# Two fused layers after attention: the next batch's attention laid beside the first product instead of the second, and weights converted in another order

## The chip, the cores and the metric

The kernel runs on one core of a Trainium2 chip. Its time is the device time of one execution in microseconds (us); the time before is 1533.37 us, the median of three runs (1531.82 to 1533.52). Engines: TensorE (PE) multiplies matrices into PSUM banks, VectorE (DVE) and ScalarE (ACT) do elementwise work, GpSimd (POOL) and SyncE (SP) here mostly issue DMAs. Each engine runs its instructions in order; between engines there are semaphores.

## The reference

Attention without softmax for 8 batches of 8 heads, 576 positions, 64 wide; then each row is divided by its root mean square and scaled by g. The result, as 4608 tokens of 512 values, goes through two layers with a hidden width of 2048:

```python
kv = np.einsum('bhsd,bhse->bhde', k, v)
out = np.einsum('bhsd,bhde->bhse', q, kv)
rms = np.sqrt(np.mean(out * out, axis=-1, keepdims=True) + 1e-06)
x = (out / rms * g_norm)                      # reshaped to (4608, 512)
h = x @ w_in;  x = (h * sigmoid(1.702 * h)) @ w_out      # layer 1
h = x @ w2_in; x = (h - np.tanh(h)) @ w2_out             # layer 2
```

All of it is float32.

## The kernel before

**Groups.** The tokens are worked in eight groups of 576, and a group of layer 1 is one batch of the attention. A group has two stages: `m1` (M1, x times W_in, activation) and `m2` (M2, times W_out). Both compute a product of 2x2 blocks by seven products of sums of blocks (the letter r in the code), so x, the weights and the hidden values are needed in seven forms. Each number is split in a high and a low float16, and each product is three matrix products (high-high, high-low, low-high). M1 has 54 steps of six matrix products of 288 columns, and two more steps of it (the tails) stand behind the first two steps of M2; M2 has 28 steps of twelve. Groups 0 and 1 of layer 1 use plain products (`m1_plain`, and `m2_plain` for group 0), while the weights of layer 1 are still being converted.

**Work on the other engines.** In M1 ScalarE copies bank X to `mscratch` (L664) and applies the activation (L638, L642), and VectorE adds the banks Y and Z to the copies (L669). For M2 the hidden values become operands `jt`: sums on VectorE (L692), the high part on ScalarE (L706), the low part on VectorE (L712), up to seven operands ahead of TensorE. At the end of a product M2 scales bank X (ScalarE, L760) and adds Y or Z (VectorE, L754); results go to memory from `mscratch`, which has room for six buffers of 288 columns. The weights of M2 stream in on SP's queue.

**Side work.** Besides that there are generators, from which `tick` takes pieces: after each step of M1 or M2 a generator's rate is added up, and for each full 1 its next piece (up to a `yield`) is put into the program. `drain` takes what is left. TensorE and SP run in the written order; the order on the other engines is decided by the scheduler, by its own estimates, no earlier than the marks at which a piece was put in. The generators are:

- `front(b)`: the attention products of batch b on TensorE (k times v, L425; times q, L434; the sums of squares, L441) with ScalarE's copies, squares (L467) and scaled copies (L468), then the roots (`roots`, L507 and L508, with a change of ScalarE's function table and back).
- `back(b)`: two steps on the roots (`newton`, L513 and L514), the roots out to memory (L556) and back, spread over 64 partitions each (L564), the multiplication (L571), then `xprep`: x in seven forms (L336), high parts (ScalarE, L346), low parts (VectorE, L349), into `xo[b % 2]`.
- `conv1`: 32 items, W_out of layer 2 first (16 items), then W_in. An item loads raw words (GpSimd's queue, L144 and L145), makes float32 of them (ScalarE L156, then VectorE L159 to L162), sums (L171 to L174), high parts (ScalarE, L224, 896 columns), low parts (VectorE, L177) and stores them (L229, L232). Two raw buffers take turns.
- `x2load`: x of layer 2, read back and prepared by the same `xprep`.

k, v and q of a batch come by GpSimd's queue (L380): k and v into a region with room for one piece of 1280 words, so the next of four pieces waits for the products that read the one before.

**Where they stand.** In M1 of group n (2 to 6) runs `back(n+1)` at 0.5, in M2 of groups 2 to 5 `front(n+2)` at 0.75; group 1 has all of batch 2 and the products of batch 3. `conv1` begins in M2 of group 2 at 0.85 and runs from group 3 at 0.62 in M1 and 0.5 in M2; it must be drained ahead of M2 of group 7, where `reload` brings W_in of layer 2 in. GpSimd's queue issues in order: the loads of k and v, the roots and the conversion's loads and stores all pass it.

## Time and profile before

| | us |
|---|---|
| median of three runs | 1533.37 |
| profiled execution | 1537.64 |
| its span | 1535.7 |
| PE busy in it | 1441.6 (94%) |
| DVE busy | 1159.7 (76%) |
| ACT busy | 892.7 (58%) |

The profile is one execution; its stages can be told apart by the lines of the products (L631 to L633 in M1, L817 to L819 in M2). A row of the table of stages gives the stretch, its length and the busy time of each engine in it; a row of the order of time gives start, duration, engine, line, operation, and in brackets how long the engine had been idle and what released it. PEclk is the mean granted clock of TensorE as a share of its higher level. Busy time of TensorE counts the pipelined ends of its products, so what a gap costs is best read from a stage's length.

### The profile page before, as it was taken

To read this page: it belongs to the slowest core of one execution; us is meant where nothing else is said; L and a number is where in the kernel's file an instruction comes from. 1 tells how busy PE (TensorE), PEld (TensorE's weight loads), DVE (VectorE), ACT (ScalarE), POOL (GpSimd) and SP (SyncE) were. 2 spreads that over 40 slices of the span, in tenths; PEclk is the share of its full clock that TensorE was granted. 3 is DMA by queue.
4 is the path that set the end of the run, shared out by engine and by line. 5 is a ranking of instruction groups with operands and counts; after the bars stand their busy time and mean duration, and the time that the engine had idled before them with its cause. 6 is when DMAs were issued, how large, how long until landed. Compare 5 with 4: busy or idle time off the path is not lost.

```text
span 1535.7 us, 29954 instructions
## 1 busy us (share of the span) xinstructions
PE 1441.6 (94%) x11922; PEld 1112.7 (72%) x11922; DVE 1159.7 (76%) x2237; ACT 892.7 (58%) x1871; POOL 152.5 (10%) x238
## 2 busy tenths in 40 slices
PE   6999978998899889998999999999999999999999
PEld 5667756676666666766777777777777777777777
DVE  3998878394885976967978686887778787868585
ACT  5775554664765756747656564645565555656463
POOL 0001010102322222111110000000000000000000
PEclk9999999999999999999999999999999999999999
DMA  8776836437477387384586516061523334240504
GB/s 285 220 239 192 249 92 203 129 115 249 125 238 226 90 269 225 124 287 131 178 292 228 181 34 222 14 203 39 171 85 132 124 104 136 71 154 31 194 15 155
DMA packets 104684, 247.55 MB, mean 161 GB/s; under 512 B 10624, under 2 KB 55296, under 8 KB 104544
## 3 DMA queue, kind: packets, MB, share of 16 engines
q1 hardware_dynamic: 83504, 161.49, 32.6%
q0 software_dynamic: 21040, 84.15, 17.4%
q8 instruction: 93, 1.52, 0.4%
q14 instruction: 47, 0.39, 0.1%
HBM read 202.62 MB, written 42.98 MB: 160 GB/s over the span
## 4 chain that ended last, share of the span: by engine, by line
PE 45%; DVE 19%; issue 19%; DMA 11%; ACT 5%; POOL 1%; SPq 0%; DVEq 0%; ACTq 0%; POOLq 0%
PE X L817 4%; PE X L818 4%; PE X L819 4%; PE X L631 3%; PE X L632 3%; PE X L633 3%; DVE gt L692 3%; DVE jt L712 3%; DMA scratch<-rd 2%; PE Y L817 2%; PE Y L819 2%; PE Y L818 2%; PE Z L631 2%; PE Z L633 2%; PE Z L632 2%
## 5 line engine op out<-in xcount | busy, mean ns | idle before, releaser
L706 ACT ACTIVATE jt<-gt 128x576 f16<-128x576 f32 x420 | 284.5, 682 | 179.7 <-PE X L819 73.6
L712 DVE SCALAR_TENSOR_TENSOR jt<-gt,jt 128x576 f16<-128x576 f32 x420 | 312.9, 753 | 95.9 <-ACT jt L706 92.8
L817 PE MATMUL X<-jt,st 128*128 128x288 f16 x960 | 278.6, 290 | 16.8 <-ACT mscratch L760 14.8
L818 PE MATMUL X<-jt,st 128*128 128x288 f16 x960 | 278.4, 290 | 3.7 <-DVE jt L712 3.7
L819 PE MATMUL X<-jt,st 128*128 128x288 f16 x960 | 278.1, 290 | 0.0
L631 PE MATMUL X<-xo,wi 128*128 128x288 f16 x896 | 256.8, 287 | 19.5 <-ACT mscratch L664 17.8
L632 PE MATMUL X<-xo,wi 128*128 128x288 f16 x896 | 256.8, 287 | 0.0
L633 PE MATMUL X<-xo,wi 128*128 128x288 f16 x896 | 256.7, 286 | 0.0
L632 PEld LDWEIGHTS <-wi 128*128 128x128 f16 x1568 | 153.6, 98 | 83.1 <-issue 43.5
L818 PEld LDWEIGHTS <-st 128*128 128x128 f16 x1680 | 165.9, 99 | 60.6 <-issue 18.5
L817 PEld LDWEIGHTS <-st 128*128 128x128 f16 x1680 | 165.8, 99 | 55.8 <-issue 11.6
L819 PEld LDWEIGHTS <-st 128*128 128x128 f16 x1680 | 165.9, 99 | 52.4 <-issue 9.1
L631 PEld LDWEIGHTS <-wi 128*128 128x128 f16 x1568 | 153.7, 98 | 41.1 <-issue 1.8
L633 PEld LDWEIGHTS <-wi 128*128 128x128 f16 x1568 | 153.7, 98 | 39.3
L664 ACT COPY mscratch<-X 128x288 f32<-128x288 f32 x336 | 130.7, 393 | 80.3 <-PE X L633 63.6
L692 DVE TENSOR_TENSOR gt<-gt 128x576 f32<-128x576 f32 x240 | 175.7, 749 | 0.6
L631 PE MATMUL Z<-xo,wi 128*128 128x288 f16 x448 | 128.3, 286 | 16.0 <-DVE mscratch L669 15.6
L818 PE MATMUL Y<-jt,st 128*128 128x288 f16 x480 | 138.1, 288 | 3.3 <-DVE jt L712 3.3
L817 PE MATMUL Y<-jt,st 128*128 128x288 f16 x480 | 138.3, 288 | 0.7 <-DVE mscratch L669 0.5
L819 PE MATMUL Y<-jt,st 128*128 128x288 f16 x480 | 138.3, 288 | 0.0
L669 DVE TENSOR_TENSOR mscratch<-Z,mscratch 128x288 f32<-128x288 f32 x224 | 101.3, 452 | 46.7 <-ACT mscratch L664 23.6
L633 PE MATMUL Z<-xo,wi 128*128 128x288 f16 x448 | 128.4, 287 | 0.0
(240 smaller groups left out, 2482.1 us busy)
## 6 DMA issues: line engine op xcount, KB each, us to landing
st<-wod SPq DMA_DIRECT2D x210, 512.0 KB, 4.8
scratch<-atp POOLq DMA_DIRECT2D x28, 640.0 KB, 6.1
scratch<-x2d SPq DMA_DIRECT2D x32, 288.0 KB, 5.6
cbk<-w_out POOLq DMA_DIRECT2D x32, 256.0 KB, 3.9
cbk<-w_in POOLq DMA_DIRECT2D x32, 256.0 KB, 3.8
scratch<-atp POOLq DMA_DIRECT2D x14, 576.0 KB, 5.5
scratch<-rd POOLq DMA_DIRECT2D x28, 288.0 KB, 6.3
x2d<-mscratch SPq DMA_DIRECT2D x28, 288.0 KB, 5.5
```

The source lines that it names most:

```text
L631: nc.tensor.matmul(out=out, lhsT=wh, rhs=xh, start=fresh and kt == 0, stop=False, skip_group_check=k)
L632: nc.tensor.matmul(out=out, lhsT=wh, rhs=xl, start=False, stop=False, skip_group_check=k)
L633: nc.tensor.matmul(out=out, lhsT=wl, rhs=xh, start=False, stop=kt == 1, skip_group_check=k)
L664: main(nc.scalar.copy(out=b.ap, in_=x))
L669: main(nc.vector.tensor_tensor(out=b.ap, in0=add[0], in1=b.ap, op=ALU.add))
L692: tt = lambda o, a, b: main(nc.vector.tensor_tensor(out=G[:, :, o, :], in0=G[:, :, a, :], in1=G[:, :, b, :], op=ALU.subtract))
L706: main(nc.scalar.activation(out=j[:, :, 0, :], in_=GT[STEPS2[i][1]][:, :, QD[STEPS2[i][0]], :], func=AF.Copy, scale=SX))
L712: main(nc.vector.scalar_tensor_tensor(out=j[:, :, 1, :], in0=GT[STEPS2[i][1]][:, :, QD[STEPS2[i][0]], :], scalar=SX, in1=j[:, :, 0, :], op ...
L817: nc.tensor.matmul(out=out, lhsT=wh, rhs=xh, start=a, stop=False, skip_group_check=k)
L818: nc.tensor.matmul(out=out, lhsT=wh, rhs=xl, start=False, stop=False, skip_group_check=k)
L819: nc.tensor.matmul(out=out, lhsT=wl, rhs=xh, start=False, stop=z, skip_group_check=k)
```

## The change

- `front` is split into `front_early` (batches 1 and 2, as before) and a new `front` for batches 3 to 7, which has the products and squares alone, with ScalarE's squares and copies in halves of 288 columns. It runs in M1 of groups 2 to 6 at 0.5 and is drained at M1's end.
- the new `back` has the roots too, and runs in M2 of groups 2 to 6 at 1.1. Group 1 has only batch 2, at 0.75 and 0.85.
- k and v of batches 3 to 7 go into the x buffer that is idle meanwhile (`xk`, room for three pieces); q has room for two pieces instead of one.
- `conv1` takes W_in first, has its high part in two halves (eight pieces per item instead of seven) and runs at 0.2 in M2 of group 2, at 0.64 and 0.2 in groups 3 to 6, at 0.85 and 0.7 in group 7, and is drained behind M1 of layer 2's first group. Only W_in's items must be done by M2 of group 7.
- `mscratch` has room for seven buffers of 288 columns; the shared scratch is 576 words smaller.

```diff
-SCRATCH, MAIN = 6472, 7 * 256
+SCRATCH, MAIN = 5896, 7 * 288
-    rx, rs, rq, rk = (Scratch(scratch[:, a:z], z - a) for a, z in
-                      ((0, 8 * H), (8 * H, 12 * H), (12 * H, 16 * H), (16 * H, SCRATCH)))
+    rx, rs, rq0, rq1, rk = (Scratch(scratch[:, a:z], z - a) for a, z in
+                            ((0, 8 * H), (8 * H, 12 * H), (12 * H, 16 * H), (12 * H, 20 * H), (16 * H, SCRATCH)))
+    xk = [Scratch(t.rearrange("p a b c d -> p (a b c d)").bitcast(F32), 14 * H) for t in xo]
+    qs_of = lambda b: rq0 if b < 3 else rq1
+    kvs_of = lambda b: rk if b < 3 else xk[b % 2]
 def conv1():
-        items = [(kind, p, h) for kind in (1, 0) for p in range(NP) for h in range(2)]
+        items = [(kind, p, h) for kind in (0, 1) for p in range(NP) for h in range(2)]
...
-            nc.scalar.copy(out=d[:, :, 0, :], in_=B[:, 1:8])
-            yield
+            for a, b in ((0, 4), (4, 7)):
+                nc.scalar.copy(out=d[:, a:b, 0, :], in_=B[:, 1 + a:1 + b])
+                yield
...
+            converted[0] += 1
-    def front(b):
+    def front_early(b):
...
+    def front(b):
+
+        kvs, qs = [ahead[b][0]], [ahead[b][1]]
+        kvs.append((yield from unit_kv(b, 1)))
+        qs.append((yield from queries(b, 1)))
+        for kt in range(2):
+            for i in range(2):
+                kb = kvs.pop(0)
+                head_products(i, kb.ap[:, 0:1280])
+                kb.free()
+                if kt == 0:
+                    kvs.append((yield from unit_kv(b, 2 + i)))
+                yield
+                yield
...
+            for j in range(2):
+                pair_numerators(qb.ap, j)
+                yield
+                for i in range(2):
+                    nc.scalar.activation(out=sq[:, i, j], in_=AT[i][:, 0:H], func=AF.Square)
+                    nc.scalar.activation(out=og[:, i, j], in_=AT[i][:, 0:H], func=AF.Copy, scale=gsc)
+                    yield
+            qb.free()
+            pair_squares(kt, ex.ap)
+            ex.free()
+            yield
+            yield
-    def back(b, dst):
+    def back_early(b, dst):
...
+    def back(b, dst):
+
+        yield
+        yield
+        yield
+        yt[:] = (yield from rq1.need(H)), (yield from rq1.need(H))
+        roots(slice(0, P))
+        nc.scalar.activation(out=dummy, in_=yt[1].ap[:, 0:1], func=AF.Gelu_apprx_sigmoid)
+        yield
+        newton(slice(0, P))
...
+        for _ in range(5):
+            yield
+        for kt in range(2):
+            o = xbs[b, kt].ap
+            nc.vector.tensor_tensor(out=o, in0=rb[kt].ap, in1=o, op=ALU.mult)
+            rb[kt].free()
+            yield
+            ex = yield from rs.need(3 * H)
+            yield from xprep(xbs[b, kt], ex, dst[:, kt])
...
-                    bk = add_side(two(), 0.85, 0.9)
+                    bk = add_side(both(2, xo[0]), 0.75, 0.85)
                 elif n < NS - 1:
-                    bk = add_side(back(n + 1, xo[(n + 1) % 2]), 0.5, 1.0)
+                    fr = add_side(front(n + 1), 0.5, 0.0)
...
             if (l, n) == (0, 3):
-                rate(later, 0.62, 0.5)
+                rate(later, 0.64, 0.2)
+            if (l, n) == (0, 7):
+                rate(later, 0.85, 0.7)
...
-                add_side(later, 0.0, 0.85)
+                add_side(later, 0.0, 0.2)
             jcap[0] = 5
+            if (l, n) == (1, 0):
+                drain([later])
             pre = [stream(l, i) for i in range(4)]
-            if l == 0 and 1 < n < NS - 2:
-                drain([bk])
-                fr = add_side(front(n + 2), 0.0, 0.75)
+            if l == 0 and 1 < n < NS - 1:
+                drain([fr])
+                bk = add_side(back(n + 1, xo[(n + 1) % 2]), 0.0, 1.1)
             if l == 0 and n == NS - 1:
-                drain([later])
+                while converted[0] < 16:
+                    next(later)
```

The order of VectorE at the multiplication by the roots of batch 5, before. It stands in M1 of group 4: L669 adds the banks, L177 and L174 are conversion, L712 is an operand's low part, L336 a form of x.

```order
L669 TENSOR_TENSOR mscratch<-Y_85,mscratch 128x288 [waits PE_49]
L174 TENSOR_TENSOR cbk<-cbk 128x128 [waits DVE_49]
L669 TENSOR_TENSOR mscratch<-Z_87,mscratch 128x288 [waits DMAHW6_49,DMAHW2_49,Activation_49]
L571 TENSOR_TENSOR scratch<-scratch 128x1152 [waits DMASW5_49,DMASW4_49]
L177 TENSOR_TENSOR cbk<-cbk 128x7x128 [waits DMASW3_49,Activation_49]
L712 SCALAR_TENSOR_TENSOR jt<-gt_73,jt 128x2x288 [waits Activation_49]
L336 TENSOR_TENSOR scratch<-scratch 128x288 [waits DVE_49]
L712 SCALAR_TENSOR_TENSOR jt<-gt_73,jt 128x2x288 [waits Activation_49]
L669 TENSOR_TENSOR mscratch<-Z_87,mscratch 128x288 [waits PE_49]
```

The same of the changed kernel, in M2 of group 4: L645 is the multiplication, L783 an operand's low part, L825 M2's addition, L162 to L165 conversion, L343 a form of x and L356 its low part.

```order
L783 SCALAR_TENSOR_TENSOR jt<-gt_75,jt 128x2x288 [waits Activation_49]
L783 SCALAR_TENSOR_TENSOR jt<-gt_76,jt 128x2x288 [waits Activation_49]
L783 SCALAR_TENSOR_TENSOR jt<-gt_73,jt 128x2x288 [waits Activation_49]
L162 TENSOR_SCALAR cbk<-cbk 128x512
L645 TENSOR_TENSOR scratch<-scratch 128x1152 [waits DMASW5_49,DMASW4_49]
L163 SCALAR_TENSOR_TENSOR cbk<-cbk 128x512 [waits DMASW3_49,DVE_49]
L783 SCALAR_TENSOR_TENSOR jt<-gt_74,jt 128x2x288 [waits Activation_49]
L825 SCALAR_TENSOR_TENSOR mscratch<-Z_86,mscratch 128x288 [waits Activation_49]
L645 TENSOR_TENSOR scratch<-scratch 128x1152 [waits DMASW7_49,DMASW6_49]
L343 TENSOR_TENSOR scratch<-scratch 128x288 [waits DVE_49]
L825 SCALAR_TENSOR_TENSOR mscratch<-Z_87,mscratch 128x288 [waits Activation_49]
```

The multiplication, and x behind it, moved from among M1's additions to among the operands of M2; seven low parts stand directly ahead of it there.

The order of ScalarE in the first half of M2 of group 4, before: L706 is an operand's high part, L443, L426 belong to the products of batch 6, L224 and L156 to conversion, L760 is M2's scaled copy.

```order
L443 ACTIVATE ms<-AT,eps 128x288 [waits PE_49]
L224 CAST cbk<-cbk 128x7x128 [waits DMASW1_49,DMASW2_49,DVE_49,Activation_49]
L706 ACTIVATE jt<-gt_74 128x2x288 [waits PE_49]
L426 COPY kv_104<-AT 128x64 [waits PE_49]
L156 ACTIVATE cbk<-cbk 128x512 [waits DMASW3_49,DMASW2_49,DVE_49]
L760 ACTIVATE mscratch<-X_82 128x288 [waits PE_49]
L760 ACTIVATE mscratch<-X_83 128x288 [waits PE_49]
```

In the changed kernel (L777 the high part, L545, L546 and L626 the roots and the way back to the activation's table, L831 the scaled copy, L159 conversion):

```order
L545 ACT_TABLE_LOAD
L545 ACTIVATE scratch<-ms 128x288
L546 ACTIVATE scratch<-scratch 128x288 [waits Activation_49]
L777 ACTIVATE jt<-gt_75 128x2x288 [waits PE_49]
L626 ACT_TABLE_LOAD
L626 ACTIVATE dummy<-scratch 128x1 [waits Activation_49]
L777 ACTIVATE jt<-gt_76 128x2x288 [waits DVE_49,PE_49]
L777 ACTIVATE jt<-gt_73 128x2x288 [waits DVE_49,PE_49]
L777 ACTIVATE jt<-gt_74 128x2x288 [waits DVE_49,PE_49]
L831 ACTIVATE mscratch<-X_82 128x288 [waits PE_49]
L831 ACTIVATE mscratch<-X_83 128x288 [waits PE_49]
```

The start of a conversion item no longer stands ahead of the scaled copies there; the roots and the two table loads do.

## Rows read from the trace of the kernel before

**Rows 1.** Busy by stretch: us, PE, PEld, DVE, ACT, POOL, PEclk, DMA share, GB/s.
```profile
146.30:272.50 126.20, 106.24 (x920) 76.85 (x919) 103.98 (x202) 64.72 (x130) 12.04 (x21) 0.97 0.62 186
272.50:380.80 108.30, 99.38 (x867) 72.11 (x866) 65.48 (x121) 62.19 (x129) 13.29 (x21) 0.95 0.51 162
380.80:691.80 311.00, 282.12 (x2402) 208.98 (x2401) 235.92 (x459) 194.34 (x396) 73.55 (x109) 0.97 0.63 197
485.90:532.50 46.60, 40.18 (x320) 31.00 (x319) 36.29 (x76) 32.97 (x75) 10.90 (x16) 1.00 0.45 133
532.50:591.80 59.30, 53.97 (x485) 38.69 (x483) 41.22 (x78) 30.95 (x56) 14.55 (x21) 0.94 0.77 249
738.50:781.10 42.60, 42.60 (x350) 34.02 (x349) 37.57 (x70) 23.97 (x41) 6.48 (x10) 1.00 0.67 214
781.10:824.70 43.60, 40.52 (x327) 31.70 (x325) 31.35 (x65) 30.12 (x72) 6.24 (x11) 1.00 0.78 276
867.30:907.20 39.90, 39.90 (x327) 31.75 (x325) 30.69 (x67) 24.28 (x61) 0.00 (x0) 1.00 0.18 56
949.80:1284.50 334.70, 330.49 (x2690) 262.89 (x2689) 257.44 (x497) 187.37 (x401) 11.42 (x16) 1.00 0.36 117
1284.50:1324.20 39.70, 39.70 (x326) 31.65 (x324) 30.63 (x67) 24.24 (x61) 0.72 (x1) 1.00 0.13 42
```

**Rows 2.** The same for the attention's bank AT alone: PE, PEld, DVE, ACT.
```profile
532.50:591.80 59.30, 7.46 (x128) 3.80 (x128) 0.46 (x1) 6.46 (x13) 0.94 0.77 249
```

**Rows 3.** Waits of PE in M2 of group 4: us, times, longest.
```profile
PE X L817 <- ACT mscratch L760: 5.3, 1, 5.3
```

**Rows 4.** Order of time of ACT around that wait.
```profile
566.70 0.66 ACT L156 ACTIVATE cbk<-cbk 128x512 f32<-128x512 f32 x1 [5.64 <-DMA cbk<-w_out]
567.26 0.70 ACT L760 ACTIVATE mscratch<-X 128x288 f32<-128x288 f32 x2
```

**Rows 5.** Busy by stretch, right behind that wait.
```profile
566.70:573.20 6.50, 5.49 (x24) 3.37 (x24) 4.39 (x10) 2.51 (x5) 1.42 (x2) 0.50 0.41 139
```

**Rows 6.** Order of time of the roots in M1 of group 4.
```profile
486.45 1.28 ACT L507 ACT_TABLE_LOAD   x1
487.75 0.44 ACT L507 ACTIVATE scratch<-ms 128x288 f32<-128x288 f32 x1
488.83 1.28 ACT L482 ACT_TABLE_LOAD   x1
...
491.62 0.56 POOL L556 DMA_DIRECT2D rd<-scratch  x1 [0.49 <-DVE scratch L514]
495.61 2.46 POOL L564 DMA_DIRECT2D scratch<-rd  x4 [3.44 <-PE Z L633]
...
501.84 1.36 DVE L571 TENSOR_TENSOR scratch<-scratch 128x1152 f32<-128x1152 f32 x1 [3.96 <-DMA scratch<-rd]
```

**Rows 7.** Waits of PE in M1 of group 4.
```profile
PE Z L631 <- DVE mscratch L669: 3.6, 2, 3.3
PE X L631 <- ACT mscratch L664: 2.6, 3, 1.4
```

**Rows 8.** VectorE by line: count, busy us, mean ns, idle before.
```profile
L712 DVE SCALAR_TENSOR_TENSOR jt<-gt,jt 128x576 f16<-128x576 f32 x420 | 312.9, 753 | 95.9 <-ACT jt L706 92.8
L336 DVE TENSOR_TENSOR scratch<-scratch 128x288 f32<-128x288 f32 x112 | 47.1, 449 | 0.2
L177 DVE TENSOR_TENSOR cbk<-cbk 128x896 f16<-128x896 f32 x32 | 34.8, 1089 | 17.0 <-ACT cbk L224 16.7
L160 DVE SCALAR_TENSOR_TENSOR cbk<-cbk 128x512 uint32<-128x512 uint32 x42 | 28.9, 688 | 0.9
L171 DVE TENSOR_TENSOR cbk<-cbk 128x128 f32<-128x128 f32 x40 | 11.4, 284 | 0.3
```

**Rows 9.** The read-back of the roots (L564), from issue to landing.
```profile
DMA to landing us min/median/max: 4.0/6.3/9.6
```

**Rows 10.** Waits of ACT from 949.8 to 1284.5 (layer 2).
```profile
ACT mscratch L664 <- DMA outT<-mscratch: 11.5, 4, 3.6
```

## What was predicted, before the changed kernel was run

> **What bounds the kernel now.** I read the table of stages first, then the waits of TensorE, then the order of time around the longest of them. Group n is the 576 tokens of turn n; M1 and M2 are its two matrix products. In the table [rows 1] the reader is to see what a stage costs when nothing holds TensorE. The first M1 of the second layer shown, 1284.5 to 1324.2, takes 39.7 us with TensorE busy all of it, and M2 of group 6 in the first layer takes 42.6 us, also without a gap. So a pair costs 82.3 us of bare products. The attention of one batch, all of which lies in M2 of group 4, adds 7.46 us of small products [rows 2].
>
> Groups 3 to 5 of the first layer take 311.0 us, 103.7 each [rows 1], where 82.3 + 7.5 = 89.8 would do: 14 us a pair are lost. Group 4 shows where. Its M1 lasts 46.6 us instead of 39.7, 6.9 too long; its M2, which holds the products of batch 6, lasts 59.3 instead of 50.1, 9.2 too long. VectorE is busy 36.29 of 46.6 and 41.22 of 59.3, ScalarE 32.97 and 30.95: neither is full, so the loss is waiting in order, not work.
>
> In M2 there is one wait of 5.3 us, of a product for ScalarE's copy [rows 3], and the order of time tells why [rows 4]: the activation that starts a conversion item (L156) stood 5.64 us for its words from memory, and the copy that TensorE needs (L760) stood behind it. The price is not 5.3 alone: in the 6.5 us after it the granted clock reads 0.50, the lower of the two levels (1.2 GHz), where TensorE had stood idle, and 24 products take 5.49 us [rows 5]; at the full level they take about 2.9 (42.60 us for 350). In M1 the roots stand at the start: two table loads of 1.28 us each with the roots between them [rows 6], behind which the copies of X come late (2.6 us, [rows 7]), and then the multiplication by the roots (L571) holds VectorE 3.96 us for the read-back [rows 6], which TensorE feels as 3.6 us [rows 7].
>
> **The change, part by part.**
>
> *Groups 2 to 6.* The products of batch n+1 go beside M1 of group n, its roots, scaling and x beside M2. Per pair the products stay 7.5 us. M1 loses the two table loads, the roots and the read-back, so the waits of [rows 6, 7] go; M2 loses the conversion's rush (0.2 pieces per step instead of 0.5, 28 steps: 5.6 pieces, under one item of 8) and the products.
>
> M1 after: VectorE gives up two multiplications of 1.36 us [rows 6], two steps of 0.45 for the roots, eight subtractions of 0.449 and x's low parts (six of 0.753, two of 0.449) [rows 8]: 12.6 us. It takes on conversion: 0.64 x 54 steps / 8 = 4.3 items where 0.62 x 54 / 7 = 4.8 were issued; nothing more. ScalarE gives up the loads, the roots and x's high parts (some 8 us) and takes the 13 instructions of [rows 2], 6.46 us, of which eight are now split in two, at some 0.1 us more a half: about 7.5. So ScalarE stays near 33 and VectorE falls below 30, in a stage that is 7.5 us longer. What is late next there is ScalarE in order: a pair's second product waits until the first one's squares and copies are out of the AT banks, one call (two steps, 1.7 us) earlier in the program. The nearest stage is M1 of group 7, 43.6 us, 3.9 over the bare 39.7, with ScalarE at 30.12 and VectorE at 31.35 [rows 1]. Bounds: 0 (M1 of group 8 has 39.9) and 6.9 (group 4). I take 3.5.
>
> M2 after: the order puts the work of the roots and of x on VectorE among 22 low parts. The sum of the wide ones is 32 x 0.753 = 24.1, ten narrow ones 4.5, the 12.6 from above, and one item of conversion: 1.089, two of 0.688, four of 0.284 and one smaller one, 4.0 [rows 8]. That is 45.2. The same sum for M2 of group 6 (32 wide, 10 narrow, 28 of conversion) gives 42.6, where the row reads 37.57 busy [rows 1], since neighbours overlap: a factor 0.88. So 40 us of 42.6: it fits, but only just, and a wait of VectorE shows. Two are added. The roots end on ScalarE some 11 us into M2 (fourth call at 1.1 per step, after the two tail steps of M1) and VectorE comes to them at about that time. Then the read-back: the write's issue of 0.56 us and its landing, four loads whose issue takes 2.46 us [rows 6], and their landing, 6.3 us in the middle and 4.0 to 9.6 at the ends [rows 9]. In M1 of group 4 the multiplication starts 10.2 us after the write's issue (501.84 - 491.62, [rows 6]); I take 10, 8 to 14. Between the end of the roots and the multiplication VectorE has 8 to 10 us of work by the order, so the wait is 0 to 2 us in the middle, 5 at the worst; queued behind it are the low parts, of which the order has six or seven in store (8 to 9 us of TensorE), and x, which the next M1 needs at once. Behind the multiplication stand some 19 us of VectorE's work, so x is complete about 24.5 + 19.2 = 43.7 us after M2's start, 1 late. Bounds: 0 (group 6) and 9.2 (group 4). I take 2.
>
> A pair is then 82.3 + 7.5 + 3.5 + 2.0 = 95.3. Groups 3 to 5: 311.0 to 285.9, -25.1. Group 2: 108.3 to 95.8 (half a microsecond more, as its x now comes late in group 1), -12.5. Group 6 had no products: 781.1 - 691.8 = 89.3 becomes 95.3, +6.0.
>
> The Trainium skill, page ScalarE: Activation LUTs, section What ACT_TABLE_LOAD costs, has a switch of tables cost about 2.66 us, a load of 1283 ns and a drain of 1380. The load agrees with this trace's 1.28 [rows 6]; the drain does not show: the root starts 0.02 us after the first load's end (487.75 against 486.45 + 1.28). By the page the two switches would put the roots 2.8 us later into M2, and each of five pairs up to that much later, 14 in all; by the rows nothing.
>
> *k and v in the idle x buffer.* Three of 1280 words fit instead of one, so the loads no longer wait in turn for the products that free the only buffer. Cost nothing: the buffer is idle until x is written, in M2. Unlike before, the loads are out before M1 starts.
>
> *Group 1.* It loses batch 3's products (7.5 us, part of them beside VectorE's backlog) and its waits for them: 126.2 to 118.0, -8.2; bounds 0 and -15, since VectorE is busy 103.98 of it [rows 1] and its floor stays.
>
> *Conversion at the end.* Pieces: 4 + 32 x 8 = 260. Up to group 6 5.6 + 4 x 40.2 = 166 are issued; M1 of group 7 takes 46, its M2 20, and the rest, 28, falls to M1 of the second layer's first group. M1 of group 7: 31.35 + (5.7 - 2) x 4.0 x 0.88 = 44.4 of VectorE, over the 39.7 of TensorE, plus what it waits: 43.6 to 46.6, +3.0 (0 to +6). The next M1: 30.69 + 3.5 x 4.0 x 0.88 = 43.0, 39.9 to 43.7, +3.8 (+1 to +7).
>
> *One more buffer (seven of 288 instead of six).* In the second layer ScalarE waits 11.5 us in four places for an output to leave mscratch [rows 10]; four pairs take 334.7 where 4 x 82.3 = 329.2 would do [rows 1]. With seven, the buffer of the last output comes round four steps (about 3 us) later, and the longest wait was 3.6. I take -5.2 (0 to -5.5).
>
> Sum: -25.1 - 12.5 + 6.0 - 8.2 + 3.0 + 3.8 - 5.2 = -38.2. From the profiled execution's 1537.6 that gives 1499.4; the median of the runs shown is 4.2 lower, so 1495.
>
> **Rivals.**
> 1. *M1 becomes the place that waits.* For: products of a batch, squares, and 4.3 items now share it, and ScalarE runs in order; the wait of [rows 4] can move there. Against: clock and memory are quieter in M1 (DMA share 0.45 against 0.77 in M2 of group 4 [rows 1]). M1's rest is 7 instead of 3.5: 5 x 3.5 = 17.5, 1512.
> 2. *The rest nearly vanishes.* For: M2 of group 6 with 37.57 of VectorE and no gap. 1 a pair instead of 5.5, 5 x 4.5 = 22.5: 1473.
> 3. *The x chain in M2 is too long: slower.* VectorE is nearly full there, x is written last, and all of M1 waits for it. If the read-back lands 10 us later than I count (its own slowest landing, the write behind the k and v loads on the same queue), M2 is 9.5 longer: 1495 + 47.5 = 1542. For: the share of 0.77. Against: the slowest landing seen is 9.6 [rows 9], 3.3 over the middle. It decides from x about 10 us after M2's last product: -38.2 is gone at 7.6 more a pair.
> 4. *GpSimd's DMAs held up by VectorE.* Each of the five issues of the chain waits for one VectorE instruction of 0.75 to 1.35: 3.8 to 6.8 us later, M2 3.5 longer, 1512. For: VectorE is busiest in M2. Against: the landing spread [rows 9] was taken beside a VectorE that was 78% busy. The Trainium skill, page SBUF — State Buffer, section SBUF: two separate sides, states such a rule: descriptors of a DMA from GpSimd's queue can't be written while VectorE runs a two-port mode. No row here shows such a wait by itself.
>
> **How the numbers follow.** Forecast 0.56, rival 1 0.18, rival 2 0.14, rival 3 0.09, rival 4 0.03. A measurement of this kernel can tell 0.2%, 3 us, from no change. Rival 3 is slower; a strong form of rival 1 may end within 0.2%, 0.03; the rest is faster: 0.88. The forecast's own range is 1482 to 1508 (a pair's rest 3 to 8). The range reaches to rivals 1 and 2: 1474 to 1520.
>
> **What would show it.** M1 of groups 3 to 6 near 50.7 and M2 near 44.6, both without the lower clock level; no wait of ScalarE for words in M2; VectorE's wait at the multiplication under 3 us; the four waits of [rows 10] gone; M1 of group 7 and of the next near 46 and 44. Wrong: x late by more than 5 us at M1's start, or M1 above 55.

## The result, and the profile after

The changed kernel takes 1540.42 us (median of 18 runs) where the kernel before takes 1531.84 beside it: ratio 1.0057, 95% interval 1.0042 to 1.0072. It is 0.57% slower, and the forecast of 1495 was wrong in sign. The profiled execution has a span of 1542.1 us against 1535.7.

The table of stages of the kernel after, with the columns of [rows 1]: group 1; groups 3 to 5 together; M1 and M2 of group 3; M2 of group 4; M1 of group 7; M1 and M2 of the second layer's first group; four pairs of the second layer.

```profile
144.20:262.00 117.80, 99.47 (x857) 73.92 (x855) 103.72 (x202) 61.56 (x123) 12.13 (x21) 1.00 0.66 201
365.40:671.10 305.70, 280.38 (x2402) 208.75 (x2401) 218.08 (x414) 188.44 (x424) 48.43 (x78) 0.97 0.57 182
365.40:416.10 50.70, 48.18 (x454) 34.60 (x453) 31.68 (x66) 34.68 (x91) 8.44 (x13) 1.00 0.31 102
416.10:468.30 52.20, 44.81 (x351) 34.91 (x349) 41.73 (x76) 27.97 (x51) 7.71 (x13) 0.93 0.82 257
518.80:569.00 50.20, 44.75 (x351) 34.55 (x349) 36.98 (x64) 25.71 (x46) 7.70 (x13) 0.97 0.79 247
771.80:818.70 46.90, 41.87 (x327) 32.51 (x325) 36.07 (x79) 31.77 (x78) 14.11 (x21) 0.96 0.81 282
863.00:908.60 45.60, 41.50 (x326) 32.42 (x325) 40.99 (x95) 31.39 (x75) 8.93 (x13) 0.96 0.36 108
908.60:960.10 51.50, 44.74 (x350) 34.77 (x349) 36.90 (x66) 23.56 (x43) 3.65 (x5) 0.93 0.56 188
960.10:1289.50 329.40, 329.40 (x2689) 262.90 (x2688) 257.74 (x497) 187.74 (x401) 11.41 (x16) 1.00 0.37 120
```

The reader is to see that M1 came out as forecast (50.7) and M2 did not: 52.2 and 50.2 where 44.6 was written down, for 42.6 of products. Over groups 2 to 6 the M1 stages grew from 235.6 to 256.4 and the M2 stages shrank only from 273.1 to 253.4, so the move of the products gave and took nearly the same.

Group 3 shows where M2 lost it. The waits in its M2, one of TensorE, one of ScalarE and one of VectorE (total, times, longest); the answer to [rows 3]:

```profile
PE X L888 <- ACT mscratch L831: 7.4, 1, 7.4
...
ACT xo L353 <- DVE scratch L645: 8.0, 1, 8.0
...
DVE scratch L645 <- DMA scratch<-rd: 5.8, 1, 5.8
```

They are one chain, read from right to left and upwards: the read-back of the roots is late, VectorE's multiplication by them (L645) stands 5.8 us for it, ScalarE's first conversion of x (L353) stands 8.0 us for the multiplication, and the copy that frees TensorE's bank (L831) stands behind that conversion in ScalarE's order. The order of time of GpSimd's queue and of the multiplication, with what ended the idle time before; the answer to [rows 6]:

```profile
429.57 0.45 DVE L552 SCALAR_TENSOR_TENSOR scratch<-scratch 128x288 f32<-128x288 f32 x1
430.32 0.55 POOL L631 DMA_DIRECT2D rd<-scratch  x1 [8.67 <-DVE scratch L552]
434.84 2.48 POOL L638 DMA_DIRECT2D scratch<-rd  x4 [1.38 <-DMA rd<-scratch]
445.62 1.36 DVE L645 TENSOR_TENSOR scratch<-scratch 128x1152 f32<-128x1152 f32 x1 [5.84 <-DMA scratch<-rd]
```

From the write's issue to the multiplication it is 445.62 - 430.32 = 15.3 us, where M1 of the kernel before needed 10.2 (from the end of VectorE's newton step, L552, it is 15.6, which the expectations below quote). Of the 5.1 us more, 4.6 lie behind the issue of the loads: 10.8 from there to the multiplication instead of 6.2 [rows 6]. Over all groups both halves land later, the write (first line) and the loads (second line, which answers to [rows 9]):

```profile
DMA to landing us min/median/max: 2.5/4.6/8.0
...
DMA to landing us min/median/max: 6.5/9.6/12.8
```

ScalarE in the same stretch, the answer to [rows 4]; the conversion of x takes the place that the conversion of the weights had there:

```profile
438.33 0.68 ACT L777 ACTIVATE jt<-gt 128x576 f16<-128x576 f32 x1 [0.73 <-PE X L890]
447.01 0.68 ACT L353 ACTIVATE xo<-scratch 128x576 f16<-128x576 f32 x1 [8.00 <-DVE scratch L645]
447.60 0.67 ACT L777 ACTIVATE jt<-gt 128x576 f16<-128x576 f32 x1
448.18 0.69 ACT L831 ACTIVATE mscratch<-X 128x288 f32<-128x288 f32 x2
```

And the table for ten microseconds during the loads, and for the stretch after TensorE's wait, where the granted clock is at the lower level again, as in [rows 5]:

```profile
435.00:445.00 10.00, 6.23 (x51) 4.84 (x50) 4.78 (x8) 2.05 (x3) 3.75 (x6) 1.00 0.97 276
445.90:452.70 6.80, 4.08 (x18) 2.51 (x18) 6.80 (x12) 4.52 (x9) 0.77 (x2) 0.50 0.61 188
```

The DMA engines are busy 0.97 of the time in which the roots come back. That share alone does not make the loads late: in M1 of group 5 of the kernel before it was 0.86 while the roots of batch 6 were loaded, and the loads landed in 5.6 us (median). What differs is whose transfers they are. The table for those loads before; then, before and after, the queues with their packets, MB and share of the engines' time (q0 is GpSimd's queue, q1 SyncE's), and the loads' size and median landing:

```profile
601.00:609.20 8.20, 8.12 (x66) 6.24 (x64) 6.47 (x13) 5.82 (x13) 3.01 (x5) 1.00 0.86 250
...
q0 software_dynamic: 524, 2.04, 85.9%
...
scratch<-rd POOLq DMA_DIRECT2D x4, 288.0 KB, 5.6
```

```profile
q0 software_dynamic: 529, 2.08, 52.8%
q1 hardware_dynamic: 746, 2.04, 45.7%
...
scratch<-rd POOLq DMA_DIRECT2D x4, 288.0 KB, 10.7
```

In M1 GpSimd's queue had the engines to itself; in M2 of group 3 (434.8 to 449.5) SyncE's queue, which brings the weights and stores results, takes nearly half of their time.

Over M2 of groups 2 to 6 VectorE's longest waits at L645 are 7.1, 5.8, 9.6, 3.9 and 5.6 us, and the stages have 11.1, 9.6, 7.6, 4.9 and 7.4 over 42.6. What TensorE stood for was not everywhere the same: the copy L831 in groups 2, 3 and 6 (8.5, 7.4 and 5.7 us), low parts (L783) in group 4 (5.3 us), weights in group 5 (2.9 us).

The second loss is at the border of the layers. The first group of layer 2 takes 97.1 us where it took 82.4. TensorE's waits there, and what SyncE's weight loads stood for:

```profile
PE Y L888 <- DMA st<-wod: 6.5, 1, 6.5
PE X L702 <- ACT mscratch L831: 4.1, 1, 4.1
...
SPq L804 <- DMA wod<-cbk: 45.1, 2, 32.6
```

W_out of layer 2, now converted last, is stored so late that the loads of M2's weights wait for the stores.

### The profile page after: what moved, and what is told of

Its sections match the earlier page's. It is cut to its first block, busy times and chain, and to the rows that moved or that the text cites. A ratio compares the mean times of both kernels' runs of the same rounds, so it can differ in the third digit from the quotient of the medians.

```text
span 1542.1 us, 30058 instructions
## 1 busy us (share of the span) xinstructions
PE 1440.5 (93%) x11922; PEld 1112.3 (72%) x11922; DVE 1161.3 (75%) x2237; ACT 896.4 (58%) x1943; POOL 152.7 (10%) x238
## 4 chain that ended last, share of the span: by engine, by line
PE 59%; DVE 17%; DMA 12%; ACT 5%; issue 5%; POOL 1%; SPq 0%; DVEq 0%; ACTq 0%; POOLq 0%
PE X L702 6%; PE X L704 6%; PE X L703 6%; PE X L888 5%; PE X L889 5%; PE X L890 5%; DMA scratch<-rd 3%; DVE jt L783 3%; PE Z L702 3%; PE Z L703 3%; PE Z L704 3%; PE Y L888 3%; PE Y L890 3%; PE Y L889 3%; DMA wod<-cbk 2%
## 5 line engine op out<-in xcount | busy, mean ns | idle before, releaser
L783 DVE SCALAR_TENSOR_TENSOR jt<-gt,jt 128x576 f16<-128x576 f32 x420 | 312.0, 752 | 99.5 <-ACT jt L777 96.2
L777 ACT ACTIVATE jt<-gt 128x576 f16<-128x576 f32 x420 | 283.0, 682 | 163.1 <-PE X L890 57.7
L888 PEld LDWEIGHTS <-st 128*128 128x128 f16 x1680 | 165.8, 99 | 59.0 <-DMA st<-wod 15.7
L890 PEld LDWEIGHTS <-st 128*128 128x128 f16 x1680 | 165.9, 99 | 55.6 <-issue 12.4
L888 PE MATMUL Y<-jt,st 128*128 128x288 f16 x480 | 139.3, 290 | 10.8 <-DMA st<-wod 9.2
```

The costliest lines, as they stand in the source:

```text
L777: main(nc.scalar.activation(out=j[:, :, 0, :], in_=GT[STEPS2[i][1]][:, :, QD[STEPS2[i][0]], :], func=AF.Copy, scale=SX))
L783: main(nc.vector.scalar_tensor_tensor(out=j[:, :, 1, :], in0=GT[STEPS2[i][1]][:, :, QD[STEPS2[i][0]], :], scalar=SX, in1=j[:, :, 0, :], op ...
L888: nc.tensor.matmul(out=out, lhsT=wh, rhs=xh, start=a, stop=False, skip_group_check=k)
L890: nc.tensor.matmul(out=out, lhsT=wl, rhs=xh, start=False, stop=z, skip_group_check=k)
```

## The experiments

Sums over stages of each run's own trace (us), M1 and M2 over groups 2 to 6, with the ratio to the kernel before measured beside it:

| kernel | M1 | M2 | group 7 | layer 2, group 0 | ratio (95%) |
|---|---|---|---|---|---|
| before | 235.6 | 273.1 | 86.2 | 82.4 | 1 |
| after | 256.4 | 253.4 | 91.1 | 97.1 | 1.0057 (1.0042-1.0072) |
| no trip | 252.0 | 217.8 | 91.7 | 95.7 | 0.9791 (0.9761-0.9821) |
| roots from SyncE | 251.1 | 279.3 | 88.3 | 97.9 | 1.0180 (1.0148-1.0212) |
| q, k, v from SyncE | 251.7 | 260.4 | 88.2 | 96.9 | 1.0066 (1.0040-1.0093) |
| roots from ScalarE | 268.7 | 234.6 | 93.9 | 95.6 | 1.0040 (1.0021-1.0059) |
| multiplication later | 261.6 | 240.8 | 92.5 | 97.9 | 0.9999 (0.9978-1.0020) |
| roots in M1 | 272.1 | 220.2 | 90.1 | 97.9 | 0.9983 (0.9961-1.0005) |
| conversion 0.80 | 263.8 | 243.0 | 93.9 | 82.3 | 0.9998 (0.9977-1.0019) |
| roots in M1, 0.80 | 275.9 | 220.9 | 94.7 | 82.3 | 0.9920 (0.9893-0.9947) |
| before, 7 buffers | 231.9 | 267.9 | 85.6 | 82.3 | 0.9933 (0.9909-0.9957) |
| spread by TensorE | 252.0 | 258.0 | 90.8 | 96.6 | 1.0066 (1.0040-1.0091) |
| the same, 0.78 | 252.7 | 257.2 | 87.9 | 82.5 | 0.9976 (0.9961-0.9990) |
| the same, copied, later | 253.7 | 226.4 | 87.7 | 82.7 | 0.9762 (0.9734-0.9789) |

**The trip taken out.** The multiplication takes what stands in its buffer.

```diff
-        nc.gpsimd.dma_start(out=rd[b], in_=t.ap)
...
-            for c in range(2):
-                nc.gpsimd.dma_start(out=t.ap[c * HD:(c + 1) * HD, :]...,
-                                    in_=rows[2 * kt + c].partition_broadcast(HD))
```

> The kernel after, but the multiplication by the roots in M2 takes what stands in its buffer: the write of the roots to memory and the four loads that bring them back are left out (so the exchange of the roots between partitions is not done from batch 3 on). Theory A, the trip through memory is late and ScalarE's copies for TensorE stand behind the conversion of x that waits for it: VectorE's waits of 4 to 10 us at the multiplication go, and with them 5 to 8 us of what M2 of groups 2 to 6 has over its products (11.1, 9.5, 7.5, 4.9, 7.4, together 40); the sum falls to 10 to 18 and the time by 20 to 32, to some 1510 to 1520. Theory B, VectorE and ScalarE are simply full in M2 and the trip only fills slack that would be lost anyway: the waits move to VectorE's and ScalarE's work, the sum stays over 28, and the time is less than 12 under the kernel after. In both, M1 and M2 of the second layer's first group (5.9 and 8.9 over their products) stay as they are.

Measured: 1503.52 us, 37 under the kernel after. M2 of group 3:

```profile
408.70:453.00 44.30, 42.75 (x350) 34.00 (x349) 41.49 (x76) 28.04 (x51) 4.69 (x8) 1.00 0.82 275
```

Theory A, and more than it expected: M2 lost 35.6 of the 40.4 us that it had over its products. VectorE has the same work (41.49 of 44.30 busy) and fits. So theory B falls, and the trip is nearly the whole loss of M2. The run takes away the trip's transfers too, not only the wait for them; it does not tell the two apart.

**Why the trip is long: three other queues.** First the roots from SyncE, then q, k and v from SyncE, then the roots from ScalarE.

```diff
-        nc.gpsimd.dma_start(out=rd[b], in_=t.ap)
+        nc.sync.dma_start(out=rd[b], in_=t.ap)
...                                                # and the four loads
```

> The kernel after with the roots' write and read-back of batches 3 to 7 issued from SyncE's queue instead of GpSimd's. If GpSimd's queue is what makes the trip long (its loads of k and v ahead of it, or its issues held up by VectorE), the trip of group 3 falls from 15.6 us to some 8 to 11, VectorE's waits at the multiplication to 0 to 3, and the time by 12 to 25. If the memory's load is what makes it long, the trip stays at 14 or more and the time within 6 of the kernel after. If SyncE's weight loads, which wait for their buffers, stand ahead of it in order, the trip becomes longer than 15.6 and the time up to 20 longer.

Measured: 1562.52 us, 22 over the kernel after, a little more than the last theory allowed, but not because the trip is longer. SyncE stands for VectorE's newton step with the weight loads behind it, and TensorE waits for weights; these are the waits in M2 of group 3, and after them the landing of the writes:

```profile
PE Z L888 <- DMA st<-wod: 10.5, 1, 10.5
...
SPq L631 <- DVE scratch L552: 9.7, 1, 9.7
```

```profile
DMA to landing us min/median/max: 1.7/1.7/1.8
```

The trip is short here, but beside a weight stream that its own wait had held up: the DMA share is 0.50 from 430 to 440 us. It does not tell queue from load.

```diff
-        nc.gpsimd.dma_start(out=t.ap[:, 0:n], in_=atp[b - 1, kt, :, a:a + n])
+        (nc.sync if b > 3 else nc.gpsimd).dma_start(...)
```

> The kernel after with the loads of q, k and v of batches 4 to 7 from SyncE's queue, in the order in which they are written, so that they no longer stand ahead of the roots' write on GpSimd's queue at M2's start. If these loads (three of some 0.65 MB beside the weight streams) are what makes the trip of the roots long, the trip falls to 9 to 12 us, VectorE's wait at the multiplication to 0 to 4, and M2 of groups 3 to 6 by 3 to 6 each, 12 to 24 in all. If the weight streams alone fill the memory, the trip stays at 14 to 16 and the time within 5 of the kernel after; the loads then delay weights on their own queue, and a wait of TensorE for those would show it.

Measured: 1545.07 us, and the loads land as late as in the kernel after, although no load of q, k or v is under way while they run. The trip of group 3 is shorter (12.4 us), but M2 of groups 2 to 6 is 7.0 longer in sum, so the loads of q, k and v are not what made M2 long. The landing of the loads:

```profile
DMA to landing us min/median/max: 6.8/9.5/13.1
```

```diff
-        nc.gpsimd.dma_start(out=rd[b], in_=t.ap)
+        (two steps later) nc.scalar.dma_start(out=rd[b], in_=t.ap)
+        (four steps later) the four loads by nc.scalar.dma_start
```

> The kernel after with the roots' write and the four loads issued from ScalarE's queue, the write two steps after VectorE's newton step, the loads four steps later, the multiplication four steps after them. It tells why the trip is long. If GpSimd's queue is slow beside a busy VectorE, the write lands in 1.5 to 2.5 us instead of 4.6 (median) and the loads in 5 to 7 instead of 9.6, with the weight streams running. If the memory's load is what makes it long, they land in 3.5 to 5.5 and 8.5 to 11 as in the kernel after. The time: ScalarE may stand for the landing of the write before it can issue the loads, with the copies for TensorE behind it; 1525 to 1550.

Measured: 1537.87 us. From ScalarE's queue the write and the loads land no earlier than from GpSimd's:

```profile
DMA to landing us min/median/max: 2.8/5.2/6.7
...
DMA to landing us min/median/max: 5.8/10.6/15.4
```

So it is not GpSimd's queue; what both queues have beside them is SyncE's. VectorE's waits stay 26.1 us in sum. M2 became 18.8 shorter and M1 12.3 longer; 7.0 us of that TensorE waits for x (L353, L356). The multiplication also stands later in the order here, and what that did is not told apart.

**The place in the order.**

```diff
-        for _ in range(5):
+        for _ in range(9):
             yield
```

> The kernel after with nine steps instead of five between the issue of the read-back and the multiplication by the roots, so that the multiplication and the conversions of x stand some 3.6 us (four steps at 1.1 per step) later in the order, and the conversion of x behind one copy for TensorE instead of ahead of it. Theory A (the wait itself is harmless, the place of the conversion ahead of the copies is not): VectorE's waits fall by 3 to 4 us, TensorE's waits of 5.7 to 8.5 for the copy go or fall by as much, and M2 of groups 2 to 6 loses 3 to 5 each, 15 to 25 in all. Theory B (x is the last thing and all is late behind it): x is complete 3 to 4 later, M1 of groups 3 to 7 waits for it at its start by as much as M2 gains, and the time stays within 6 of the kernel after.

Measured: 1532.75 us, half of each theory. In M2 12.6 us are gained, in M1 5.2 given back; TensorE's waits for x in M1 are 5.6 us over groups 3 to 6, where the kernel after has 2.3. VectorE's wait over M2 of groups 2 to 6 did not fall: the row of the kernel after, and that of this run.

```profile
DVE scratch L645 <- DMA scratch<-rd: 34.4, 8, 9.6
```

```profile
DVE scratch L645 <- DMA scratch<-rd: 35.8, 5, 10.3
```

The later place in the order did not help VectorE, which runs through its order ahead of its time and then stands. What it changed is who stands behind it: TensorE's waits for the copy L831 fell from 21.6 in three groups to 9.0 in one.

```diff
-                fr = add_side(front(n + 1), 0.5, 0.0)
+                fr = add_side(front_trip(n + 1), 0.65, 0.0)   # front, then roots, write and loads
```

> The kernel after with the roots, the write and the loads of the read-back at the end of the products' program (0.65 of its steps per step of M1 instead of 0.5), so that they fall into the last quarter of M1 and only the multiplication and x stay beside M2. Theory A (the trip through memory and its place are what cost): the trip is over at M2's start, M2 of groups 2 to 6 has 0 to 4 over its products instead of 11.1 to 4.9, M1 takes two table loads and 0 to 2 us more each; together 20 to 33 less than the kernel after, 1508 to 1521, under the kernel before (ratio 0.984 to 0.993). Rival: the table loads stand ahead of ScalarE's copies in M1 as in the kernel before and cost 4 or more there each, 20 in all, and x in M2 is still late: 1530 or more.

Measured: 1529.88 us. The trip is hidden, M2 has 7 us in five groups over its products; but M1 gave back 15.7, more than the 0 to 10 of theory A, less than the 20 of the rival, and the time is over theory A's 1521. Landing of the write and of the loads, from GpSimd's queue, now beside M1; the table for the write and for the loads of batch 5 in M1 of group 4; and ScalarE's table loads there:

```profile
DMA to landing us min/median/max: 2.0/2.0/2.6
...
DMA to landing us min/median/max: 3.9/6.2/9.6
```

```profile
504.80:507.00 2.20, 2.20 (x20) 1.75 (x19) 2.20 (x5) 1.76 (x5) 1.11 (x2) 1.00 0.17 67
507.40:516.60 9.20, 9.20 (x76) 7.24 (x75) 7.57 (x18) 6.48 (x15) 5.51 (x9) 1.00 0.90 255
```

```profile
497.64 1.28 ACT L545 ACT_TABLE_LOAD   x1
498.94 0.44 ACT L545 ACTIVATE scratch<-ms 128x288 f32<-128x288 f32 x1
499.29 0.38 ACT L737 COPY mscratch<-X 128x288 f32<-128x288 f32 x1
499.68 1.28 ACT L711 ACT_TABLE_LOAD   x1
```

Beside a VectorE busy all of the 2.20 us the write lands in 2.0 again, and at a DMA share of 0.90 the loads land in 6.2, as in [rows 9]. The same queue is quick in M1 at nearly the share at which it is slow in M2; GpSimd's queue alone takes 0.89 of that 0.90. The two table loads stand among the copies that TensorE needs. How much of the 15.7 is theirs was not measured alone.

**The conversion.**

```diff
-                rate(later, 0.64, 0.2)
+                rate(later, 0.80, 0.2)
```

> The kernel after with the conversion in M1 of groups 3 to 6 at 0.80 pieces per step instead of 0.64: 4 x 54 x 0.16 = 35 pieces, 4.3 items, done earlier, more than the 28 pieces that fall to M1 of the second layer's first group. Theory C (W_out's last items are late because they are issued late): M1 of that group falls from 5.9 over its products to 0 to 2, M2 from 8.9 to 0 to 2, and M1 of groups 3 to 6 becomes 0 to 2 longer each: 6 to 13 less than the kernel after. Rival D (M2's wait there is the order of SyncE's queue, whose weight loads stand behind the last stores wherever they come from): M2 keeps 6 or more and the time is within 4 of the kernel after.

Measured: 1531.17 us, ratio 0.9998. The first group of layer 2 is back at bare products; M1 and M2 in that order:

```profile
864.90:904.60 39.70, 39.70 (x326) 31.65 (x325) 30.69 (x67) 24.30 (x61) 0.00 (x0) 1.00 0.17 55
904.60:947.30 42.70, 42.70 (x351) 34.12 (x349) 33.83 (x59) 22.72 (x41) 2.14 (x3) 1.00 0.54 180
```

Theory C; D falls. M1 of groups 2 to 6 took back 7.4, at the upper end of what was expected, 5.7 of it in group 4. That M2 of groups 2 to 6 became 10.4 shorter was not expected, and why it did stays open.

Both edits together, the roots in M1 and the conversion at 0.80:

```diff
+                fr = add_side(front_trip(n + 1), 0.65, 0.0)
+                rate(later, 0.80, 0.2)
```

> The roots in M1's last quarter and the conversion at 0.80 together. By theories A and C the gains add up, since they lie in different stages: 26 to 46 less than the kernel after, 1495 to 1514, ratio to the kernel before 0.976 to 0.989. If ScalarE and VectorE in M1 can't take both (the rate and the roots), M1 of groups 3 to 6 is 3 or more longer than in the run with the roots alone and the sum stays 10 under the two gains.

Measured: 1519.45 us, 21 under the kernel after. The two gains as measured, 10.5 and 9.2, add up, and M1 (275.9) is under 1 us a group longer than with the roots alone; the range was too high by what the roots in M1 had been given.

**The buffers alone.** The edit is to the kernel before.

```diff
-SCRATCH, MAIN = 6472, 7 * 256
+SCRATCH, MAIN = 5896, 7 * 288
```

> The kernel before with one part of the change alone: seven buffers of mscratch instead of six. If ScalarE's four waits for outputs to leave mscratch (11.5 us) are lost only to the six buffers, M1 of the second layer falls from 40.8-41.7 to 39.7 as in the kernel after, and the time by 4 to 5.5 (ratio 0.9965 to 0.9975). If the waits come from memory that the kernel after loads less there, they stay and the time too (ratio 0.999 to 1.001).

Measured: 1522.32 us, ratio 0.9933: 9.0 under the runs beside it, more than the 4 to 5.5. Four pairs of layer 2:

```profile
939.00:1268.50 329.50, 329.50 (x2690) 262.91 (x2689) 258.04 (x497) 187.84 (x401) 11.41 (x16) 1.00 0.37 120
```

They take 329.5 where [rows 1] has 334.7, as expected; M1 and M2 of groups 2 to 6 are 8.9 shorter in this trace. The spans of the two traces differ by 15.6 and the medians by 9.0, so how much of those 8.9 is the buffers stays open. Against this version the rest of the change costs, by the ratios, 1.0057 - 0.9933, some 19 us, not 9.

**The roots without memory.** TensorE spreads the roots over the partitions, as batch 0 does, into the two banks that M2 leaves free.

```diff
-        nc.gpsimd.dma_start(out=rd[b], in_=t.ap)   # and the four loads
+        yield from halves(slice(0, P), yt[0].ap.bitcast(F32R), hl0)
+        (for each kt, i:)
+                for j in range(2):
+                    nc.tensor.matmul(out=AT[j][:, 0:H], lhsT=spread[:, 2 * i + j, kt, :], rhs=hl0, ...)
+                nc.vector.tensor_tensor(out=o, in0=at2[:, :, 0:H], in1=o, op=ALU.mult)
```

> The kernel after without the trip through memory, but with the exchange done: the roots are split in two halves (one cast on ScalarE, one instruction on VectorE), TensorE spreads them over the partitions into the two free AT banks (eight products per pair, in four rounds of two), and four multiplications from there of two banks each (some 0.75 us) take the place of two of 1.36. Theory A (the trip is what M2 lost; M2's VectorE has room for some 1 us more): M2 of groups 2 to 6 has 1 to 4 over its products and some 2.5 to 3.5 us of spreading, where the kernel after has 11.1 to 4.9: sum 18 to 35 instead of 40, so 5 to 22 less than the kernel after, 1518 to 1535, best value 1523. Rival: TensorE, which runs in order, waits in the four rounds for VectorE to free the AT banks, 1 to 2 us each, and M2 keeps 8 or more a pair: no gain.

The side work of M2 runs at 1.2 pieces per step here instead of 1.1. Measured: 1543.00 us, no gain. Not the rival's waits, but one before the first of the four rounds; TensorE's waits from group 2 to group 6:

```profile
PE AT L636 <- DVE hl L559: 27.2, 5, 6.6
```

VectorE reaches the roots some 5 us after their place in the order, and TensorE, in order, stood for it.

```diff
-                rate(later, 0.64, 0.2)
+                rate(later, 0.78, 0.2)
```

> The same with the conversion in M1 of groups 3 to 6 at 0.78 pieces per step. The loss of the second layer's first group (14.8 over its products in the kernel after) goes as in the run with the conversion alone, and M1 takes 1 to 2 each: 5 to 10 under the run without it, 1508 to 1530; ratio to the kernel before 0.985 to 0.999.

Measured: 1528.47 us, ratio 0.9976, 14.5 under the run without it: more than the 5 to 10, as layer 2's first group is back at 82.5 and M1 takes 0.7 in five groups for it.

```diff
+        for _ in range(10):          # before the first spreading product, instead of 2
+            yield
-                nc.vector.tensor_tensor(out=o, in0=at2[:, :, 0:H], in1=o, op=ALU.mult)
+            nc.scalar.copy(out=rb[kt] part, in_=at2[:, :, 0:H])   # and one multiplication per kt
```

> The run with the roots spread by TensorE and the conversion at 0.78, with the two places mended at which TensorE waited or would wait: the spreading stands eight steps later in the order than there (at 1.3 instead of 1.2 steps), behind the 4.4 to 6.6 us by which VectorE's half of the roots came late, and ScalarE, which has room in M2, copies the banks out, so that they do not wait for VectorE. If the wait at the first spread product was all that was left of the loss, M2 of groups 2 to 6 has 1 to 4 over its products and 1.7 of spreading, and the time is 15 to 28 under the run without these two, 1500 to 1514; ratio to the kernel before 0.979 to 0.989. If VectorE is simply late in M2 by 5 us, the wait moves to x at the start of the next M1, which becomes 3 to 5 longer, and the time stays at 1520 or more.

Measured: 1497.23 us, ratio 0.9762, 31 under the run without the two, a little more than the 15 to 28 expected. M2 of group 3 and M1 of group 4, and TensorE's wait in the spreading, groups 2 to 6:

```profile
408.70:453.70 45.00, 43.96 (x358) 35.01 (x357) 42.61 (x77) 29.90 (x55) 5.94 (x10) 1.00 0.82 271
453.70:505.20 51.50, 48.02 (x454) 34.66 (x453) 34.50 (x71) 36.42 (x94) 9.18 (x14) 1.00 0.36 119
```

```profile
PE AT L623 <- ACT scratch L625: 5.2, 5, 1.0
```

M2 is 45.0 with VectorE busy 42.61 of it and eight more products, at the full clock; from group 2 to group 6 TensorE has no wait for x. Which of the two edits gave how much was not measured. This version beats both kernels and the kernel before with seven buffers.

## Why the prediction was wrong, point by point

- **M1 of groups 2 to 6: right.** 3.5 over the products was written down, 50.7 a stage; groups 3, 4 and 6 have 50.7, 50.5 and 50.7. What is late next is near what was named: TensorE stands for ScalarE's squares and copies (L515), 1.2 us at a pair's second product (L441) and 4.7 at the sums of squares behind it (L448), over groups 3 to 6. Group 5 has 54.6; TensorE waits 2.3 us there for x.
- **M2: the step that failed.** "I take 10, 8 to 14" for the read-back was a duration read beside M1, where SyncE's queue takes 0.3% of the DMA engines' time during the trip, and carried to M2, where it takes nearly half. It took 15.3 in group 3. The shares that the prediction set side by side, 0.45 and 0.77, are means of whole stages: during the trip from which the 10 was read the share was 0.62, and the loads of batch 6 landed in 5.6 us at 0.86. The wait was then priced by what VectorE has queued behind it ("six or seven low parts in store"), and ScalarE's order was left out: there the first conversion of x waits for VectorE and TensorE's next copy for the conversion. In group 3 TensorE stood 7.4 us for that copy and not for low parts, and its granted clock was 0.50 after it, the lower level; groups 2 and 6 lost 8.5 and 5.7 in the same way. In group 4 the store did run out (5.3 us), as the prediction had feared. 2.0 a pair was written; measured are 11.1, 9.6, 7.6, 4.9, 7.4. That is 40.4 - 10 = 30 us of the some 46 between the sum (-38.2) and the result.
- **VectorE's sum: right.** 40 us busy of 42.6; without the trip it is 41.49 at the most, and M2 ends at most 2.0 us late.
- **Rival 3** (x chain too long, 1542) had the cause, a late read-back, and the place, M2. It got 0.09 because "the slowest landing seen is 9.6": that landing, too, came from M1 (of group 3). Its path was another: what ended first was not x at the end but ScalarE's order in the middle. That its time is so near is luck: it had the read-back 10 us later and all of the 47.5 us in M2, where 5.1, 30 and a loss at the border of the layers were measured.
- **Rival 4** (GpSimd's issues held by VectorE) falls: from ScalarE's queue the landings are as late. The Trainium skill's page SBUF — State Buffer, section SBUF: two separate sides, has the rule behind it, that GpSimd can't write a DMA's descriptors while VectorE runs a two-port mode; here its queue beside a VectorE busy all of 2.20 us lands the write in 2.0 us, and no run shows such a hold. Whether VectorE was in that mode there, no row tells. The 78% that the prediction set against this rival is a mean of the stage: during that trip (491.6 to 501.8) VectorE was busy 4.26 of 10.2 us.
- **Border of the layers: mis-sized.** M1 of group 7 46.9 for 46.6, M1 of the next group +5.7 for +3.8; but M2 of that group, not priced at all, lost 8.9, and M2 of group 7, not priced either, 1.7. The pieces were counted, and the chain from the last store to the weight loads was not followed. Some 13 us.
- **mscratch:** -5.2 forecast, the pairs of layer 2 gave 5.3 of 334.7. Alone the buffers give 9. **Group 1:** -8.2 forecast, -8.4 measured; the other versions of the kernel after, whose program for it is the same, have 117.7 to 120.3 there, so that the last digits agree by chance.
- In the last version, with the trip replaced and the conversion mended, M1 and M2 of groups 2 to 6 have 50.7 and 45.3 on average, where the forecast had 50.7 and 44.6. That its 1497 is so near to the forecast's 1495 is partly chance, as it is another kernel: it has products in place of the trip, and another rate of the conversion.

## What to carry to other kernels

A transfer's duration belongs to the stage in which it was measured: before a small round trip through memory is moved, look at which queues move data in the stage it goes to, not only at the DMA share, and take the time from a transfer there. When a wait is added, follow every engine that consumes behind it in order, not only the one that waits; the shortest store decides. Here, where the other engines had room, it was better to replace the round trip by an on-chip path (products into idle banks, 0.9762) than to move it (0.9920 with the conversion mended).

## What the hardware showed that was not expected

- The DMA share alone does not tell how long a transfer takes. The same four loads of 288 KB landed in 5.6 and 6.2 us (medians) at shares of 0.86 and 0.90 in M1, where GpSimd's queue had the engines nearly to itself, and in 10.7 in M2 of group 3, where SyncE's queue took 45.7% of their time; over all groups in 9.6 in M2 from GpSimd's queue and 10.6 from ScalarE's, the write in 4.6 and 5.2 instead of 2.0. That SyncE's stream is the reason is read from these rows: no run kept the trip in M2 and took the stream away. GpSimd's own other transfers can delay the loads too: batch 6 of the run with the roots in M1 has a median of 8.4 at 0.88, with next to nothing on SyncE's queue.
- From ScalarE's queue the four loads took 3.60 us of issue in M2 of group 3 and 2.7 to 3.0 in the other four groups, in the engine's own order, where GpSimd takes 2.48.
- One buffer of 1152 bytes a partition more gave 9.0 us (6.6 to 13.9 by the interval of its ratio), of which layer 2 explains some 5.
